# All chunks of a gated linear attention loaded as token pairs, with one decay sum for each pair of chunks

## The chip, the cores and the metric

The kernel runs on one core of a Trainium2 chip. The metric is the device time of one execution in microseconds (us); the median of three runs is given. The core has a matrix engine (PE, with weight loads listed apart as PEld), three engines for elementwise work (DVE, ACT, POOL), and SP, which here only issues DMA transfers. POOL can't read PSUM, where PE leaves its results.

## What is computed

A gated linear attention runs over 4 batches of 8 heads, 768 tokens and a head size of 48. Its output goes through a gated MLP that mixes along the sequence.

```python
for t in range(S):
    state = alpha[:, :, t, :, None] * state + np.einsum('bhd,bhe->bhde', k[:, :, t], v[:, :, t])
    y[:, :, t] = np.einsum('bhd,bhde->bhe', q[:, :, t], state)
...
h = np.maximum(x @ w_in, 0.0)
u, v = (h[..., :d_ff // 2].copy(), h[..., d_ff // 2:].copy())
v_n = (v - mu) / np.sqrt(var + 1e-06)
v_s = np.einsum('ts,bsd->btd', w_spatial, v_n) + b_spatial[None, :, None]
gated = u * v_s
return (gated @ w_out).astype(np.float32)
```

Here x is y with its heads joined to 384 columns, d_ff is 1024, and mu and var are taken over the 512 columns of v. Inputs and output are float32.

## The kernel before

**Chunks.** Each batch is cut into 6 chunks of 128 tokens, 24 chunks in all. Within a chunk the running product of alpha is B = exp(cumulative sum of ln alpha). With kt = k / B and qt = q * B, the scores are a plain product kt qt, masked so that a token sees only earlier ones and itself. The state between chunks is carried beside that.

**Two paths.** Chunks 0 to 7 (the tuple PAIRS names pairs 0 to 3) go through `pair` (L423), two chunks at once. Its loads (L441) put two neighbouring tokens in one partition, so that a packet has 384 bytes. The decay sum is four products of 384 columns for a pair (L461), two for the even tokens (par 0) and two for the odd ones. Each then has its own exponentials: `einvp` (L469, 1/B) and `eexpp` (L478, B, written back to PSUM). kt is L483, on POOL or DVE; qt is L490, on DVE, and reads B from PSUM. The transposes (L511) take 128 columns each.

Chunks 8 to 23 go through `first` (L634), one chunk at a time, with loads of one token to a partition in packets of 192 bytes (L646). There is one decay sum (L666) with four narrow products for the total decay (L669), one pair of exponentials (L678, L695), kt (L690, POOL), qt (L700, DVE, from PSUM), and transposes of 64 columns (L719).

Both paths then do the same steps. Scores are L583 or L754 and end in PSUM, where DVE multiplies them by the mask into `ptm` (L594, L765), four products of 512 columns for each two chunks. The masked scores times v are L610 or L782, the part from the carried state L623 or L776. State updates are L553 or L740: PE multiplies kt and v, DVE adds the old state (L339), POOL multiplies by the total decay (L344), and two casts write the state's blocks `sbd` (L351, L352, recorded at L199). `finish_x` (L356) copies the output to `x_sb`, transposes it and copies it to `xT`.

**The MLP.** `second_v` and `second_u` project a batch; relu evacuates to `v_sb` and `uT`. Statistics of v are on DVE (L893, L894), or on ACT for the four chunks of ACT_STATS; `vn` (L925) normalises. `second_s` multiplies by the transposed spatial weights, DVE adds the bias into `vsb` (L976), and POOL multiplies by u into `gT` (L989; on DVE three times at the end). `second_o` is the output product; its result is copied and stored by SP. All these matrix products are recorded at L828 and all copies at L197 (ACT) or L199 (DVE and POOL).

**Order.** Nothing is scheduled at run time. Every operation is appended to a list by the function that describes it, and the string PLAN names them in the order in which they are emitted: a letter for the engine and a number for the operation. `replay` (L109) goes through it. A number after a colon asks for a filling product of so many float32 columns on PE (L187) ahead of the operation, whose result is not used. Each engine works through its own instructions in this order and waits on semaphores. PSUM banks are handed out in rotation.

Of the kernel before, what the change touches and what calls it, by code (L numbers as in the profile page):

```python
# [14 lines left out]

class Op:


    def __init__(self, key, eng, dur, emit, deps=(), prio=0.0, take=None, lat=0.13, cols=0):  # L20
        self.key = key
        self.eng = {eng: dur} if isinstance(eng, str) else dict(eng)
        self.emit, self.prio, self.lat, self.cols = emit, prio, lat, cols
        self.take = [take] if isinstance(take, Slot) else list(take or ())
        self.deps = [d for d in deps if d is not None]
        self.done = False
        self.big = False


class Ring:  # L30


    def __init__(self, bufs):
        self.bufs = bufs


class Slot:
    def __init__(self, ring):
        self.ring, self.users = ring, []


ENGINES = {
    "kt": {"POOL": 0.9},
    "vb": {"POOL": 0.48, "ACT": 0.42},
    "S": {"POOL": 0.5},
    "sb": {"POOL": 0.73, "DVE": 0.95},
    "vn": {"DVE": 0.42},
    "xe": {"ACT": 0.4},
    "ev": {"DVE": 0.34, "ACT": 0.48},
    "u": {"ACT": 0.39, "DVE": 0.49},  # L50
    "o": {"ACT": 0.4},
}
PAIRS = (0, 1, 2, 3)
ACT_STATS = ((2, 2), (1, 4))
LETTERS = {"P": "PE", "D": "DVE", "A": "ACT", "G": "POOL", "S": "SP", "Q": "DMA"}

PLAN = """
S34 Q35 S36 Q37 G32 G0 Q33 S38 Q39 S94 Q95 S40 Q41 A42 P53:512:512:192 A54 D1 D2 D56 P43 S96 Q97 S98 Q99 S100 Q101
S163 Q164 S4 Q5 S165 Q166 S167 Q168 P59:464 G58 G48 A44 A45 A55 D46 D57 D47 P249:304 P49 P61 A50 P51 D52 D60 A62 A102
A250 P71:304 P74 P113 P103 D72 D73 D76 D75 P63 P77:172 D65 A114 D116 P119:148 A104 A64 A115 A105 A78 G66 G67 G106 D107  # L60
D117 D68 P79 P81 P111 P121 P247 P109 G3 G69 A108 A82 A80 D120 D122 D112 D110 P83 A84 A171 D248 S169 Q170 S9 Q10 S307
Q308 P131 P134 D133 D136 D132 D135 G70 G118 P172:228 P182 P123:240 A183 A8 A173 A124 P137 P138 A139 A174 G7 G6 D125
P85 G126 D128 D185 G127 G129 G175 P88 P142 P140 A86 A184 D176 D186 A143 A89 P188 P190 P180 P144 P178 A141 A191 A145
A181 P146 G11 G12 S309 Q310 S311 Q312 D130 D87 D179 D90 D189 P157 A187 A177 A158 A147 A13 P197 P200 P192 D199 D201
D198 D194 D202 P151:196 P155 A315 A193 A91 P326 P316 A327 P203 P153 P204 G195 G196 G329 A317 A328 A318 P149 A205 A154
D159 D156 D152 D330 G319 P208 P334 A209 P206 D320 P332 P324 P210 P322 D92 D335 D325 D333 D148 A207 P212 A211 A150 P347
P215 P221 A213 A160 A222 A216 S14 Q15 P223 P227 S18 Q19 D93 D323 D161 D348 D349 D214 G16 G17 A224 A228 P225 P229 A226
A21 P232 A234 D231 D230 D233 G20 P235:300 P238 S313 Q314 G331 G321 P344 P336 S367 Q368 S369 Q370 S22 Q23 S371 Q372
A237 A236 D217 D162 D346 A240 D338 A239 A218 D219 D220 A375 A337 P251 P263 P259 P376 A377 A378 G339 P264 D345 D341
D265 P260 D261 P255 P252 A380 A25 A24 D381 D253 P256 D257 G340 G342 G379 S409 Q410 S373 Q374 S446 Q447 S411 Q412 S413  # L70
Q414 S415 Q416 S26 Q27 S480 Q481 S448 Q449 S482 Q483 S450 Q451 S484 Q485 P383 A385 A417 S452 Q453 S577 Q578 S486 Q487
S581 Q582 S579 Q580 S583 Q584 P244 P241 P350 A246 D384 D245 D242 D243 P390 P354 P418 D392 D391 A351 A355 G262 G343
A420 A382 G254 G266 P279 P352 P271 P356 P393 P272 A353 A357 A419 G421 A422 A394 P280 P361 P386 P275 P395 A362 A424
A396 A31 D273 D423 D281 D387 P425 D397 D427 D426 D363 G282 G388 P276 P358 D277 P398 G258 G389 G278 G30 A399 A454 A359
A28 A488 P405 P432 P267 P455 P401 A402 A457 A456 D29 P291 P489 P268 A490 A459 D406 D433 D400 D434 D360 P283 P428 D269
D460 A492 D429 D493 G458 G491 P435 A284 A292 A436 G274 G461 G270 G430 G431 S648 Q649 S617 Q618 S650 Q651 S611 Q612
S652 Q653 S613 Q614 S690 Q691 S615 Q616 S694 Q695 S654 Q655 S692 Q693 P287 P462 P437 P495 P403 D463 D464 D497 D496
A288 A439 A438 P440 A585 A441 A364 D404 P469 P498 P295 P465 P586 P303 D471 D470 D466 D500 D499 A296 A587 A588 A590
A304 P299 G494 G467 G468 G589 G592 D591 D442 P472 A473 P501 P407 P474 A502 A300 P503 P593 P596 A443 A505 A408 D475
D476 P477 A478 D504 D366 D594 D595 D445 D444 D597 D365 P506 P600 P515 D601 D516 A507 A479 A508 D509 D602 A656 A510  # L80
A619 P517 P525 P513 P519 P529 P657 P533 P620 D511 D512 P526 P530 A514 A659 A658 A621 A661 A622 A698 A624 D518 D520
D527 D531 D662 P545 P534 P699 A701 A700 A703 D625 G598 G599 G660 G626 G623 G528 D535 P546 D547 P630 P627 P664 P537
P603 D631 D665 D704 G548 A629 A628 G632 G663 A604 P538 P634 P605 S728 Q729 S762 Q763 S696 Q697 S730 Q731 S732 Q733
S764 Q765 S766 Q767 D539 A607 A666 A606 D635 D636 P541 P667 P542 G702 G532 P706 P671 D668 D543 D673 D672 G669 G536
G670 G544 G633 P608 P637 P521 A707 A736 A708 A638 P737 P713 P639 P522 P549 D714 D715 D641 D523 A770 A609 A705 A738
A739 G740 A640 A741 D742 P771 P550 P642 A772 P709 P744 A774 A643 A746 D710 D551 D775 D745 D644 G524 S858 Q859 S734
Q735 S929 Q930 S860 Q861 G773 G711 G552 G712 G743 G540 P716 P674 A717 A675 P561 P718 P676 P777 P553 A562 A678 A677
D719 D779 D720 D610 P679 P751 A778 A554 A866 A680 A645 A681 P780 D752 P747 D748 D753 D781 D782 P682 P867 P721 P754
A868 A869 A871 A722 A755 S768 Q769 S862 Q863 A723 A776 D683 D872 P573 P688 P684 G749 G750 G870 P756 P874 D646 D757
D875 D685 D758 A689 A574 D724 A876 P686 P783 P569 P881 A784 P785 A570 A787 A687 A725 D882 D786 D883 P759 P557 A760  # L90
P788 P565 P796 P798 P800 S1042 Q1043 S971 Q972 S892 Q893 S864 Q865 S898 Q899 S896 Q897 A979 A558 A789 A566 A937 A900
S894 Q895 S935 Q936 G873 S975 Q976 S931 Q932 S933 Q934 S973 Q974 S977 Q978 S1008 Q1009 S567 Q568 S1046 Q1047 S559 Q560
S1012 Q1013 S1010 Q1011 S1044 Q1045 S1014 Q1015 D727 D647 D761 D726 P794 P806 D790 A791 D799 D797 D795 D792 D793 D801
P901 P980 P802 P938 P877 P807 A902 A903 A907 A905 A981 A939 A940 A982 A944 A984 P810 P803 A942 G904 D878 G941 G879
D808 D906 D804 G805 G880 G809 G983 D985 D943 P822 P884 P811 D812 A885 P823 P908 P886 P945 D824 P814 P911 P815 D912
D909 D816 G813 G817 G913 G825 A910 A887 A888 A947 A946 P889 A1016 A890 P952 P915 P987 D953 D916 D954 P830 P1017 P831
P818 A988 A1019 A1050 A1018 D917 P948 P819 P1051 D949 A1021 A986 A989 D1022 D832 G950 P834 A1052 G951 G1020 P990 P842
P918 A835 A1054 D820 D991 D1055 A843 A919 P838 P1024 P994 P920 D1025 D921 D995 D996 A839 A1023 G914 G833 G1053 G992
S1048 Q1049 S575 Q576 S836 Q837 S844 Q845 S293 Q294 S289 Q290 S571 Q572 S305 Q306 S301 Q302 S555 Q556 A922 A1026 S297
Q298 S285 Q286 S840 Q841 P826 P955 P827 D828 A956 P1057 P957 P1031 D958 P1027 D1028 D1033 D1032 P997 P923 A1058 A1059  # L100
A959 P969 P1060 A1056 A998 P999 D1062 D1001 D1061 D970 G821 G829 G993 G1029 A1000 A924 P960 P846 P1034 A961 A847 G1030
P1063 A1035 A1064 P1002 P963 P1036 P1065 D925 D891 A1003 D962 D1066 P850 P967 A1067 A1037 D1004 A926 D928 P1068 A964
A1038 P1039 D927 D968 A851 A1005 A1069 A1040 D1006 D1041 D1007 D1070 P965 P854 P1076 P1080 P1078 P1074 D966 A1079 A855
A1071 A1081 D1075 D1072 D1073 D1077 P1094 P1082 P1106 P1086 P1083 P1098 P1095 P1090 P1102 P1087 P1107 P1091 P1103
P1110 P1099 P1111 D1096 D1084 G1085 D1088 D1097 D1108 D1092 D1093 G1089 P1113 D1104 G1109 G1105 D1112 D1100 D1101
P1117 P1121 S852 Q853 S563 Q564 S856 Q857 S848 Q849 A1114 S1115 Q1116 A1118 P1133 S1119 Q1120 A1122 P1125 A1134 S1123
Q1124 P1129 S1135 Q1136 A1126 P1137 S1127 Q1128 A1130 A1138 S1131 Q1132 S1139 Q1140
"""


def replay(ops, fill, plan):

    for word in plan.split():
        number, *junk = word[1:].split(":")
# [9 lines left out]
def kernel(  # L124
# [50 lines left out]
    def bank(shape):  # L175
# [5 lines left out]
        for x in shape[1:]:  # L181
            n *= x
# [111 lines left out]
    def op(key, *args, **kw):  # L294
# [3 lines left out]
        for s in users:  # L298
            s.users.append(o)
# [857 lines left out]
```

## Time and profile before

| | |
|---|---|
| runs | 145.87, 145.33, 145.24 us; median 145.33 |
| profiled execution, span from first to last instruction | 142.7 us |
| median less span | 2.6 us |
| last causal mask on DVE ends | 119.4 us |
| POOL idle before `gT` L989 | 14.9 us, of which 13.5 after 119 us |
| DMA | 89,000 packets, 28.64 MB, 83,728 of them under 512 bytes |
| granted PE clock | 1.00 |

The span is that of one profiled execution; what lies around it is not in the profile, and the three runs were timed apart from it. Busy time of an engine is the time in which at least one of its records is open. Records of one engine can overlap, above all PE's, so a mean duration times a count exceeds what the engine needs. Where a price is wanted, the distance from one start to the next in an unbroken row is the better measure.

### The profile page before, as it was taken

What the parts mean: (1) busy time and instruction counts of PE and PEld (TensorE: products, weight loads), DVE (VectorE), ACT (ScalarE), POOL (GpSimd) and SP (SyncE); (2) the same over time, 40 slices, a digit from 0 to 9 for tenths busy, and PEclk for the clock granted to TensorE, in tenths of its full rate; (3) what the DMA queues carried; (4) which work ended last, traced back from release to release, by engine and by line L of the source; (5) the groups of instructions that cost most, each with busy time, mean ns of one, the idle gap of its engine ahead of it and who ended that gap; (6) DMA issues with size and microseconds to landing.
All of it is one profiled execution on the core that took longest, in us unless ns stands there. A gap on an engine that the chain in (4) does not pass through costs nothing.

```text
span 142.7 us, 4968 instructions
## 1 busy us (share of the span) xinstructions
PE 134.7 (94%) x1912; PEld 84.8 (59%) x1923; DVE 118.3 (83%) x291; ACT 109.3 (77%) x282; POOL 83.4 (58%) x146
## 2 busy tenths in 40 slices
PE   7999798899999999999999999999999989999990
PEld 3457575566577656675666665656666656566560
DVE  7279878989989699999998898989979779994940
ACT  3477759999888969889987999997978978940061
POOL 6703977366339776982389999410799993000720
PEclk9999999999999999999999999999999999999999
DMA  4999999999998999999999998999998794113045
GB/s 106 270 261 261 321 259 256 290 289 358 236 217 160 237 226 202 194 169 203 171 196 183 182 198 140 214 152 194 191 231 165 229 341 168 56 58 111 0 161 170
DMA packets 89000, 28.64 MB, mean 201 GB/s; under 512 B 83728, under 2 KB 87440, under 8 KB 88976
## 3 DMA queue, kind: packets, MB, share of 16 engines
q1 hardware_dynamic: 88944, 28.32, 91.3%
q8 instruction: 15, 0.25, 0.8%
q14 instruction: 9, 0.07, 0.2%
q0 software_dynamic: 32, 0.00, 0.0%
HBM read 23.60 MB, written 4.72 MB: 198 GB/s over the span
## 4 chain that ended last, share of the span: by engine, by line
PE 63%; SPq 9%; POOL 7%; DMA 6%; DVE 5%; ACT 4%; issue 3%; ACTq 0%; POOLq 0%; DVEq 0%
PE bank L828 46%; SPq L441 8%; DMA qc<-in_q_dram 6%; PE bank L719 2%; PE bank L754 2%; POOL kt L690 2%; POOL gT L989 2%; POOL sbd L199 2%; PE bank L782 2%; DVE ptm L765 1%; PE bank L740 1%; PE bank L666 1%; SPq L1081 1%; PE bank L776 1%; DVE qt L490 1%
## 5 line engine op out<-in xcount | busy, mean ns | idle before, releaser
L828 PE MATMUL bank<-w_spT,vn 128*128 128x384 bf16 x192 | 36.8, 326 | 0.0
L989 POOL TENSOR_TENSOR gT<-vsb,uT 128x384 bf16<-128x384 f32 x28 | 25.7, 925 | 14.9 <-DVE vsb L976 14.4
L765 DVE TENSOR_TENSOR ptm<-bank,mask 128x512 bf16<-128x512 f32 x32 | 20.7, 682 | 1.9 <-PE bank L398 1.2
L828 PEld LDWEIGHTS <-vn 128*128 128x128 bf16 x192 | 16.6, 97 | 9.5 <-issue 0.2
L690 POOL TENSOR_TENSOR kt<-kc,binv 128x384 bf16<-128x384 f32 x16 | 14.6, 915 | 9.9 <-ACT bc L685 5.1
L976 DVE TENSOR_TENSOR vsb<-bank,bsp_bc 128x384 f32<-128x384 f32 x31 | 16.5, 551 | 4.2 <-PE bank L828 2.5
L828 PE MATMUL bank<-xT,w_in 128*128 128x384 bf16 x96 | 18.7, 326 | 0.0
L828 PE MATMUL bank<-w_out_sb,gT 128*128 128x384 bf16 (+1 forms) x100 | 18.7, 319 | 0.0
L828 PE MATMUL bank<-w_in,xT 128*128 128x512 bf16 x61 | 17.1, 379 | 0.8 <-issue 0.2
L344 POOL TENSOR_TENSOR state<-state,bc 128x192 f32<-128x192 f32 x20 | 10.4, 522 | 8.9 <-ACT bc L559 3.4
L197 ACT COPY kqT<-bank 128x512 bf16<-128x512 bf16 x21 | 12.1, 598 | 3.7 <-PE bank L719 1.1
L199 POOL CAST sbd<-state 64x192 bf16<-64x192 f32 x38 | 13.3, 350 | 2.0
L893 DVE BATCH_NORM_STATS2 stats<-v_sb 128x6 f32<-128x512 bf16 x20 | 13.6, 682 | 0.3 <-ACT v_sb L203 0.3
L203 ACT ACTIVATE v_sb<-bank 128x512 bf16<-128x512 f32 x20 | 11.7, 604 | 1.2 <-PE bank L828 1.0
L828 PEld LDWEIGHTS <-w_in 128*128 128x128 bf16 x96 | 8.8, 97 | 5.9
L828 PEld LDWEIGHTS <-gT 128*128 128x128 bf16 x100 | 8.9, 97 | 5.6 <-DVE gT L989 0.4
L199 DVE COPY kqT<-bank 128x512 bf16<-128x512 bf16 x27 | 10.4, 416 | 1.9 <-PE bank L511 1.0
L197 ACT CAST x_sb<-bank 128x384 bf16<-128x384 f32 x24 | 11.4, 489 | 0.7 <-PE bank L610 0.2
L187 PE MATMUL bank<-junk 128*128 128x512 f32 (+9 forms) x24 | 10.5, 542 | 1.1 <-DVE junk L240 1.1
L197 ACT COPY xT<-bank 128x192 bf16<-128x192 bf16 (+1 forms) x26 | 9.3, 376 | 1.7 <-PE bank L398 1.1
L594 DVE TENSOR_TENSOR ptm<-bank,mask 128x512 bf16<-128x512 f32 x16 | 10.2, 682 | 0.5 <-PE bank L583 0.3
L197 ACT COPY o_sb<-bank 128x384 f32<-128x384 f32 x9 | 4.4, 484 | 8.0 <-PE bank L828 8.0
(126 smaller groups left out, 285.4 us busy)
## 6 DMA issues: line engine op xcount, KB each, us to landing
ac<-in_alpha_dram SPq DMA_DIRECT2D x16, 192.0 KB, 4.4
kc<-in_k_dram SPq DMA_DIRECT2D x16, 192.0 KB, 4.9
qc<-in_q_dram SPq DMA_DIRECT2D x16, 192.0 KB, 4.3
vc<-in_v_dram SPq DMA_DIRECT2D x16, 192.0 KB, 4.4
raw_w<-in_moe_w_spatial_dram SPq DMA_DIRECT2D x3, 768.0 KB, 6.7
out_dram<-raw_w SPq DMA_DIRECT2D x11, 192.0 KB, 2.7
out_dram<-o_sb SPq DMA_DIRECT2D x9, 192.0 KB, 1.9
ac<-in_alpha_dram SPq DMA_DIRECT2D x4, 384.0 KB, 6.2
```

Of the source, the lines that this page charges most:

```text
L187: nc.tensor.matmul(out=flat[:, 0:cols].rearrange("p (a b) -> p a b", a=4), lhsT=junk, rhs=junk[:, None, 0:n].to_broadcast([128, 4, n]), st ...
L197: nc.scalar.copy(out=out, in_=in_)
L199: ENG[eng].tensor_copy(out=out, in_=in_)
L203: nc.scalar.activation(out=out, in_=in_, func=AF.Relu)
L344: ENG[eng].tensor_tensor(out=st["state"], in0=st["state"], in1=st["bc"][:, :, None].to_broadcast([128, HP, D]), op=ALU.mult)
L441: nc.sync.dma_start(out=t.rearrange("p h a d -> p h (a d)"), in_=src[b, :, t0:t0 + 2 * C, :].rearrange("h (p a) d -> p h (a d)", a=2))
L690: ENG[eng].tensor_mul(out=k_blocks(kt3)[:, :, :, 0:D], in0=quad(st["kc"]), in1=st["binv"])
L765: nc.vector.tensor_tensor(out=st["ptm"][:, s], in0=st[f"pt{s}"], in1=mask4, op=ALU.mult)
L828: return lambda ps: nc.tensor.matmul(out=out(ps), lhsT=lhsT(), rhs=rhs(), start=start, stop=stop)
L893: nc.vector.bn_stats(out=stats, in_=d["v_sb"][:, tt, :])
L976: nc.vector.tensor_tensor(out=hold["vs"], in0=ps[:, 0:TH], in1=bsp_bc[:, th, :], op=ALU.add)
L989: ENG[eng].tensor_tensor(out=bt[b]["gT"][:, dsl, cols], in0=hold["vs"], in1=bt[b]["uT"][:, dsl, cols], op=ALU.mult)
```

## The change

The path for single chunks goes. All twelve pairs of chunks are loaded as pairs, two tokens to a partition in packets of 384 bytes.

For each pair there is one decay sum. The even token's alpha is multiplied by the odd one's (`pa`), in place, and the sum runs over the logs of these products, so it gives B of the odd token. The even token's k is multiplied by the odd alpha (`ka`), and its q by the inverse of the odd alpha (`qa`), which ACT makes as exp(-ln alpha) (`ia`); after that one 1/B and one B serve both tokens. B is written to SBUF (`bexp`), no longer back to PSUM, so kt and qt can each be done on POOL or DVE.

State updates write 64x64 tiles. The sum goes to its own buffer `zs`; the decayed state for the next chunk and the two blocks `sbd` are both products of `zs` with the decay. The mask is kept once for four heads and broadcast. All statistics of v are on DVE. The order table is new, with an explicit PSUM bank for every operation that takes one (after an @).

Engines by the new order table, for the operations that move: `pa`, `ka`, `qa` 31 on POOL and 5 on DVE; kt 12 and 12; qt 14 and 10; gT 15 and 16 (and the last one on DVE from PSUM, as before); states 11 and 5; state blocks 16 and 4 (each two products); v casts 12 on POOL, 9 on ACT, 3 on DVE. Filling products come to 2,096 columns, where they were 3,572. In SP's queue the first loads stand in the order alpha 0, q 0, alpha 1, k 0, v 0, alpha 2; before, alpha 0, k 0, q 0, alpha 1, v 0.

```diff
-PAIRS = (0, 1, 2, 3)
-ACT_STATS = ((2, 2), (1, 4))
...
-S34 Q35 S36 Q37 G32 G0 Q33 S38 Q39 S94 Q95 S40 Q41 A42 P53:512:512:192 A54 D1 D2 D56 P43 S96 Q97 S98 Q99 S100 Q101
...
+S52 G4 D1 D2 S54 D0 D56 A57 G7 S109 D3 G113
+A58 P61@0:512:512:360 A62 S53 A64 G60 S55 D59 A114 D68 D65 A63
...
+            def load(_, x=x, src=src):
+                nc.sync.dma_start(
+                    out=t[x].rearrange("p h a d -> p h (a d)"),
+                    in_=src[b, :, t0:t0 + 2 * C, :].rearrange("h (p a) d -> p h (a d)", a=2))
...
+        op(("pa", j), "POOL DVE", lambda e: mul(e, t["ac"][:, :, 0, :], t["ac"][:, :, 0, :], t["ac"][:, :, 1, :]),
+           [("ac", j)])
...
+            nc.scalar.activation(out=la[:, :, :, 0:D], in_=quad(t["ac"][:, :, 0, :]), func=AF.Ln)
...
+            nc.scalar.activation(out=ia[n2], in_=t["ac"][:, :, 1, :], func=AF.Ln)
+            nc.scalar.activation(out=ia[n2], in_=ia[n2], func=AF.Exp, scale=-1.0)
...
+        op(("ka", j), "POOL DVE", lambda e: mul(e, t["kc"][:, :, 0, :], t["kc"][:, :, 0, :], t["ac"][:, :, 1, :]),
+           [("ac", j), ("kc", j)])
+        op(("qa", j), "POOL DVE", lambda e: mul(e, t["qc"][:, :, 0, :], t["qc"][:, :, 0, :], ia[n2]),
+           [("ia", j), ("qc", j)])
...
-                for p2 in range(2):
-                    nc.tensor.matmul(
-                        out=cm[:, 0:DM], lhsT=lt_pair if p2 > par else le_pair, rhs=lap[:, p2, :, 0:D],
-                        start=(p2 == 0), stop=(p2 == 1))
...
+            nc.tensor.matmul(out=cm[:, 0:DM], lhsT=le_pair, rhs=la[:, :, :, 0:D], start=True, stop=True)
...
-                nc.scalar.activation(out=cv, in_=cv, func=AF.Exp)
...
+        op(("eexp", j), "ACT", lambda _: nc.scalar.activation(out=bexp[n2], in_=sums(), func=AF.Exp),
...
-            op(("qtp", j, par), "DVE", 0.47, qtf, got(("eexpp", j, par), ("qc", 2 * j), ("cz", 0)) + tr_users("q", jo), prio=P + 4, use=[sl_c[par]])
...
+            op(("qt", j, par), "POOL DVE",
+               lambda e, par=par: mul(
+                   e, qt[:, par, :, :, 0:D], quad(t["qc"][:, :, par, :]), quad(bexp[n2])),
...
-                            out=T[i]["tp"][:, hp, :], lhsT=k_window(ktp[rows, par], hp, 2 - 2 * s),
-                            rhs=st["vb"][rows, par, 2 * hp + s, :], start=(n == 0), stop=(n == 3))
...
+                                out=tp[i][half(s), hp, :], lhsT=kt[rows, par, hp, s, :],
+                                rhs=vbp[j % 3][rows, par, 2 * hp + s, :], start=(par == 0), stop=(par == 1))
...
+                op(("S", i), "POOL DVE", lambda e, i=i, decay=decay: mul(e, state[i % 3], zs[i % 3], decay(slice(0, 128))),
...
+                    mul(e, sbd[i % NB][half(s), :, s * D:s * D + D], zs[i % 3][half(s)], decay(half(s)))
...
+                        in1=mask[:, par][:, None, :].to_broadcast([128, HP, 128]), op=ALU.mult)
...
+        spare[d] = op(("g", b, d, th), "POOL DVE",
+                      lambda e: mul(e, gT[b % 2][:, d, cols], vs[d], uT[b % 3][:, d, cols]),
```

## What the time is predicted to be, and why

> **What bounds the kernel now.** I read the page first, then busy time in two stretches that meet where DVE ends its last causal mask (119.4 us), then the chain of waits, then the groups, then single instructions.
>
> ```profile
> PE 134.7 (94%) x1912; PEld 84.8 (59%) x1923; DVE 118.3 (83%) x291; ACT 109.3 (77%) x282; POOL 83.4 (58%) x146
> ```
>
> ```profile
> 0.00:119.40 119.40, 114.79 (x1769) 73.32 (x1780) 103.14 (x257) 99.64 (x256) 79.59 (x142) 1.00 1.06 223
> 119.40:142.70 23.30, 19.89 (x149) 11.46 (x146) 15.17 (x35) 9.70 (x27) 3.85 (x4) 1.00 0.25 88
> ```
>
> The columns are the length, then PE, PEld, DVE, ACT, POOL, the granted clock (full throughout), the DMA share and GB/s. In the first stretch PE idles 4.6 us, DVE 16.3, POOL 39.8. In the second PE works alone.
>
> ```profile
> PE 63%; SPq 9%; POOL 7%; DMA 6%; DVE 5%; ACT 4%; issue 3%; ACTq 0%; POOLq 0%; DVEq 0%
> ```
>
> ```profile
> 13.96 8.82 DMA qc<-in_q_dram
> ...
> 27.72 0.50 PE bank L553 x16
> ...
> 34.43 0.35 PE bank L583 x16
> ...
> 45.44 0.47 PE bank L610 x32
> ...
> 48.23 0.20 PE bank L782 x8
> ...
> 50.94 0.23 PE bank L719 x16
> ...
> 121.48 17.55 PE bank L828 x105
> ```
>
> The chain (start, length, what) is loads until 22.8 us, then mostly PE. The last row gives 0.167 us for a matrix product of 384 columns (17.55/105), although the groups call one 326 ns: records overlap. So I price an instruction by what it adds in a row, and PE's pieces by this chain.
>
> **What PE loses.** Four pairs take the paired path now. Their four sums of 384 columns become one: 3 x 0.163 (L461, start to start) x 4 pairs = 2.0 us. Their sixteen 128-column transposes (0.056 apart, 0.90) become two sets of sixteen at 0.23: 0.44 x 4 = 1.8. The eight pairs loaded as single chunks lose one 384-column sum and four narrow ones of 0.025 each: 0.26 x 8 = 2.1. Scores (two sets of 0.35 against two of 0.33) and the masked products (0.47 against two of 0.20 plus joining) are level. That is -5.9 us. The 64x64 state products do not occur before: thirty-two of them cost 0.50 like L553's, or 0.25 if four run at once, or 0.70 at L583's pace; I take 0.50, level, with +-2.5 us over twelve pairs. Filling products go from 3,572 to 2,096 columns, but stand in idle time: nothing.
>
> The order table also moves products behind the last mask. Counted in both tables and priced as above (v 0.65, u 0.49, output 0.65, each mixing product 0.163), PE has 20.7 us left there before and 26.4 after. So it loses 11.3 us in the first stretch and gains 5.7 in the second. The second took 23.3 us, 2.6 more than its products (last store and drain); with 26.4 it takes 29.0.
>
> **What DVE has in the first stretch.** In a row a mask costs 0.60 (four take 2.48), a 384-wide product 0.47 (two qt take 1.02, one 0.55), a k/q copy 0.33, statistics 0.86. Up to the last mask it gains 8 kt, 9 gT, 5 products with alpha (22 x 0.47 = 10.3), 5 states of 192 columns (0.27 each, 1.4), state blocks 1.6, 3 v casts 0.8, 4 statistics 3.4, 2 x copies 0.9. It loses 14 qt (6.6), 9 u (4.2), 6 vsb (2.8), 8 k/q copies (2.6), 5 smaller x copies (0.8), the bias copy and the sums of ACT's statistics (1.5), memsets (0.8). The sum is -0.9, within what I can count: DVE stays at 103 us. Behind the mask it gains 6.6, under PE's cover (15.2 + 6.6 < 29).
>
> **POOL.** 31 products with alpha and 14 qt at 0.88 (a gT to the next op) add 39.6; gT falls from 22 to 8 there (-12.3), kt from 20 to 12 (-7.0), state from 19 to 11 (-3.8). State blocks become products: 32 at 0.46 (L344's price; the cast's 0.36 is the other bound) for 34 casts at 0.36, +2.5. Six more weight casts +3.9, smaller masks -3.6. Sum +19.3: POOL goes from 79.6 to 99 us.
>
> ACT ends lower: half the exponentials of the sums (-9.4 at 0.39), no squares (-3.2), fewer casts and outputs (-7), against one log and one exponential more per pair (+5), k/q copies (+4) and u (+4.5).
>
> **DMA and SP.** Thirty-two load issues and 32,768 packets go. The chain has no load after 22.8 us, and the loads before that are paired already, so this buys nothing. One order does cost: k of the first pair goes from second in SP's queue to fourth. Paired loads land about 1.5 us apart, so kt waits for it 0 to 2 us; DVE, its masks and PE's filling products are behind. I put it inside the idle time below.
>
> **The wait that the change adds.**
>
> ```profile
> 132.73 2.02 POOL L989 TENSOR_TENSOR gT<-vsb,uT 128x384 bf16<-128x384 f32 x2
> ...
> 134.08 1.09 DVE L989 TENSOR_TENSOR gT<-vsb,uT 128x384 bf16<-128x384 f32 x1
> ```
>
> ```profile
> L989 DVE TENSOR_TENSOR gT<-vsb,uT x3: 547/559/1086, 132.6 to 136.6; 128x384 bf16<-128x384 f32 x3
> ```
>
> ```profile
> L199 POOL CAST sbd<-state x38: 337/341/618, 14.6 to 118.9; 64x192 bf16<-64x192 f32 x38
> ```
>
> A DVE product with both operands in SBUF, begun while POOL's gT ran to 134.75, took 1.09 us instead of 0.55 and ended 0.42 after POOL. POOL suffers too: a cast of 618 ns beside DVE's kt at 22.0, two gT in 2.02. Before, DVE runs only 7 such products (4 kt, 3 gT), since qt (L490, L700) reads PSUM. After, the exponential goes to SBUF, and DVE has 12 kt, 10 qt, 5 with alpha, 9 gT, 5 states and 8 state blocks: 49 before the last mask. If they fall at random, POOL is running at 99/116 = 0.85 of them; the rest of a 0.88 us op is 0.44 on average, of which 0.13 hides under DVE's own start (0.55 - 0.42). That is 0.85 x 0.31 x 49 = 13 us of DVE waiting. Bounds: 0 if the order keeps them apart, 20 if every one meets a fresh op. Behind a waiting product stand masks and PSUM reads, and PE waits for those. Nearly level engines (DVE 103, POOL 99, PE 114.8 - 11.3 = 103.5 by its overlapping records) mean that a wait lands on the path about one time in three: I take 4.3.
>
> **Sum.** First stretch: DVE 103, its idle first 10 us (4.5, from the page's slices), and 4.6 of other stalls, what the fullest engine PE has now: 112.1; waits 4.3; second stretch 29.0. Span 145.4 against 142.7. The runs' median of 145.33 is 2.6 over the span, so the time is **148.0 us**, 1.8% slower.
>
> **Rivals.**
> - *The port paces.* POOL's 99 and DVE's 49 x 0.42 = 20.6 exclude each other: 119 us plus 4.5 at the start, plus 29.0: span 152.7, 155.3 us. For it: both directions of waiting are seen. Against: POOL's own 0.05 to 0.1 between reads may overlap. The Trainium skill (SBUF — State Buffer, Who interferes with whom) says that a VectorE instruction with two SBUF inputs and a GpSimd one that reads SBUF exclude each other, the second waiting in full. The row at 134.08 agrees, with 0.42 us after the other's end.
> - *The waits hide.* Products meet POOL where DVE would idle: 112.1 + 29.0 + 2.6 = 143.7. For it: DVE idled 16 us in this stretch. Against: PE paced then.
> - *PE still paces, faster.* The other engines keep up as now: 142.7 - 11.3 + 5.7 = 137.1, 139.7 us; to 137 with the cheap state products. For it: PE is 63% of the chain and DVE's first stretch is no fuller than now. It decides if DVE's idle time and waits together stay under 119.4 - 11.3 - 103 = 5 us. Against it: the start alone takes 4.5, and POOL gains 19 us and feeds kt, qt and the decay sum.
> - *Nothing visible*: gain on PE and loss on the port cancel near 145.3.
>
> **Chances.** Forecast (146.1 to 152) 0.41; port 0.15; waits hide 0.17; PE paces 0.22; cancel 0.05. A measurement here tells 0.5% (144.6 to 146.1) from no change. Of the third case 0.13 lies below 144.6, 0.03 inside, 0.01 above: faster 0.35, same 0.08, slower 0.57. The range is 137 to 154; about 0.05 lies below and 0.1 above; the forecast's own is 146.1 to 152.
>
> **What would show it.** POOL near 100 us busy and DVE near 125; PE about 120; kt, qt and gT on DVE with medians well over 0.55 us and maxima near 1.1 to 1.4, POOL's products with maxima over 1.1; the share of DVE and POOL in the chain well over today's 12%; the last mask ending near 116 and PE alone for 29 us. It is wrong if DVE's products with two SBUF inputs stay at 0.55, or if PE keeps most of the chain and the last mask ends by 108; and if the first mask comes later than 13 us (10.9 now), the load order cost more than I took.

## The result, and the profile after

The changed kernel takes **169.15 us** (median of four runs, 167.87 to 169.97) against 145.3 before: the ratio is 1.164, with a 95% interval of 1.157 to 1.171. Forecast were 148.0 us and a range of 137 to 154. The direction was right and the size far off.

The page's busy time and the chain of waits of the kernel after:

```profile
PE 140.2 (84%) x2313; PEld 84.6 (51%) x2313; DVE 147.9 (89%) x298; ACT 107.3 (65%) x272; POOL 117.1 (70%) x155
...
PE 36%; DVE 34%; POOL 13%; issue 11%; ACT 4%; DVEq 0%; POOLq 0%
```

The two stretches, which now meet at 135.54 us, where DVE ends its last causal mask (length, then PE, PEld, DVE, ACT, POOL, the granted clock, the DMA share and GB/s):

```profile
0.00:135.54 135.54, 113.17 (x2098) 68.50 (x2098) 125.61 (x249) 96.46 (x243) 110.02 (x148) 0.92 0.77 190
135.54:166.10 30.56, 27.07 (x216) 16.11 (x215) 22.28 (x50) 10.81 (x29) 7.04 (x7) 1.00 0.28 98
```

Before, DVE had 103 us of work in the first stretch and idled 16. Now it is busy for 125.6 of 135.5 us. PE's share of the chain falls from 63% to 36%, and DVE and POOL together go from 12% to 47%. The second stretch is 30.6 us, near the 29.0 that were forecast. So nearly all of the miss lies in the first, which was forecast to end at 116.4 us (112.1 and 4.3).

What DVE does with the time is seen in one kind of product. The rows give count, then minimum, median and maximum in ns, and first and last start:

```profile
L205 DVE TENSOR_TENSOR kt<-kc,binv x12: 540/806/1343, 9.9 to 103.6; 128x384 bf16<-128x384 f32 x12
L205 POOL TENSOR_TENSOR kt<-kc,binv x12: 907/1021/1233, 16.4 to 124.8; 128x384 bf16<-128x384 f32 x12
```

The cheapest kt on DVE still takes 0.54 us, as before. Half of them take over 0.8. In the timeline, a pair whose two kt fall on both engines at once:

```profile
60.51 0.91 POOL L205 TENSOR_TENSOR kt<-kc,binv 128x384 bf16<-128x384 f32 x1
```

```profile
60.57 1.26 DVE L205 TENSOR_TENSOR kt<-kc,binv 128x384 bf16<-128x384 f32 x1
```

POOL's ends at 61.42. DVE's, begun 0.06 us after POOL's, ends at 61.83, 0.41 later: the same 0.42 that the row at 134.08 showed before the change.

Two things stand beside this. The first mask starts at 18.73 us (10.93 before), and PE's clock, full throughout before, is at half speed from 13.6 to 34.0 us:

```profile
PEclk9996555599999999999999999999999999999999
```

### The profile page after: what moved, and what is told of

Its sections match the earlier page's. It is cut to its first block, busy times and chain, and to the rows that moved or that the text cites. A ratio compares the mean times of both kernels' runs of the same rounds, so it can differ in the third digit from the quotient of the medians.

```text
span 166.1 us, 5703 instructions
## 1 busy us (share of the span) xinstructions
PE 140.2 (84%) x2313; PEld 84.6 (51%) x2313; DVE 147.9 (89%) x298; ACT 107.3 (65%) x272; POOL 117.1 (70%) x155
## 3 DMA queue, kind: packets, MB, share of 16 engines
q1 hardware_dynamic: 55664, 28.32, 66.9%
## 4 chain that ended last, share of the span: by engine, by line
PE 36%; DVE 34%; POOL 13%; issue 11%; ACT 4%; DVEq 0%; POOLq 0%
PE bank L566 24%; DVE ptm L503 7%; DVE vn L645 4%; POOL qt L205 4%; DVE sbd L205 3%; PE bank L495 3%; DVE kt L205 3%; DVE vs L701 2%; DVE gT L205 2%; DVE stats L628 2%; DVE qt L205 2%; POOL sbd L205 2%; POOL qc L205 2%; PE bank L532 2%; DVE state L205 2%
## 5 line engine op out<-in xcount | busy, mean ns | idle before, releaser
L205 POOL TENSOR_TENSOR gT<-vs,uT 128x384 bf16<-128x384 f32 x15 | 14.4, 967 | 21.9 <-DVE vs L701 19.5
L205 POOL TENSOR_TENSOR sbd<-zs,bc 64x192 bf16<-64x192 f32 x32 | 18.3, 571 | 4.3 <-DVE zs L469 3.1
L205 POOL TENSOR_TENSOR qt<-qc,bexp 128x384 bf16<-128x384 f32 x14 | 15.4, 1104 | 4.2 <-ACT bexp L394 2.9
L701 DVE TENSOR_TENSOR vs<-bank,bsp_bc 128x384 f32<-128x384 f32 x31 | 16.2, 547 | 1.9 <-PE bank L566 1.7
L194 ACT COPY xT<-bank 128x192 bf16<-128x192 bf16 x38 | 12.5, 392 | 2.9 <-PE bank L553 2.6
L645 DVE TENSOR_SCALAR vn<-v_sb,mvs,rstd 128x512 bf16<-128x512 bf16 x24 | 13.2, 574 | 1.2 <-ACT rstd L639 1.2
L200 ACT ACTIVATE uT<-bank 128x384 bf16<-128x384 f32 x26 | 12.5, 492 | 1.5 <-PE bank L566 1.5
L205 POOL TENSOR_TENSOR ac<-ac 128x384 f32<-128x384 f32 x9 | 9.3, 1029 | 5.6 <-DMA ac<-in_alpha_dram 5.5
L205 POOL TENSOR_TENSOR kt<-kc,binv 128x384 bf16<-128x384 f32 x12 | 12.3, 1027 | 0.6 <-ACT binv L392 0.5
L253 PE MATMUL bank<-junk 128*128 128x512 f32 (+7 forms) x22 | 10.7, 608 | 1.8 <-DVE junk L295 1.8
L205 POOL TENSOR_TENSOR qc<-qc,ia 128x384 f32<-128x384 f32 x11 | 11.9, 1086 | 0.2
```

Source lines behind the costliest of these rows:

```text
L194: nc.scalar.copy(out=out, in_=in_)
L200: nc.scalar.activation(out=out, in_=in_, func=AF.Relu)
L205: ENG[eng].tensor_tensor(out=out, in0=in0, in1=in1, op=ALU.mult)
L253: nc.tensor.matmul(out=t[:, 0:cols].rearrange("p (a b) -> p a b", a=4), lhsT=junk, rhs=junk[:, None, 0:n].to_broadcast([128, 4, n]), start ...
L645: nc.vector.tensor_scalar(out=vn[n2][:, x, :], in0=v_sb[n2][:, x, :], scalar1=mvs[n2][:, x, 0:1], scalar2=rstd[n2][:, x:x + 1], op0=ALU.su ...
L701: nc.vector.tensor_tensor(out=vs[d], in0=banks[sl.bank][:, 0:TH], in1=bsp_bc[:, th, :], op=ALU.add)
```

## The experiments

Four theories were put to the test. A: DVE's operations and POOL's reads of SBUF exclude each other, and DVE pays for it with path time. B: the half clock and the late start. C: the new order itself, or the number of operations, whatever one costs. D: a general slowness of SBUF.

### POOL reads nothing

```diff
+        elif eng == "POOL":
+            nc.gpsimd.memset(out, 0.01)
...
-    def mul(eng, out, in0, in1):
+    def mul(eng, out, in0, in1, fill=0.01):
+        if eng == "POOL":
+            for _ in range(2):
+                nc.gpsimd.memset(out, fill)
+            return
...
```

> The changed kernel, in which every product that POOL makes is replaced by two memsets of its output (every cast on POOL by one), so that POOL reads nothing from SBUF while it stays about as busy; POOL's products and casts are left out of what is computed. Theory A, collisions of DVE's and POOL's SBUF reads make up most of the 24 us: DVE's products with two SBUF inputs fall from means of 0.74 to 0.92 us back to 0.50 to 0.60, DVE's busy time from 147.9 to about 125 us, and the time to 145 to 153 us. Theory B, the clock at half speed from 13.6 to 34.1 us and the start make up most of it: the time stays at 160 us or more, though DVE's products are shorter. Theory C, the new order itself keeps the engines apart whatever an instruction costs: DVE's busy time falls by over 15 us but the time by less than 5.

149.21 us, ratio 1.025 (1.018 to 1.033). Its two stretches, which meet at its last mask:

```profile
0.00:116.44 116.44, 109.65 (x2098) 67.97 (x2098) 104.06 (x249) 94.00 (x243) 94.65 (x270) 0.91 0.89 221
116.44:147.00 30.56, 27.06 (x216) 16.04 (x215) 22.23 (x50) 10.93 (x29) 0.00 (x0) 1.00 0.28 98
```

and its products on DVE:

```profile
L211 DVE TENSOR_TENSOR kt<-kc,binv x12: 541/548/645, 9.5 to 90.7; 128x384 bf16<-128x384 f32 x12
...
L211 DVE TENSOR_TENSOR qt<-qc,bexp x10: 523/548/552, 16.0 to 106.8; 128x384 bf16<-128x384 f32 x10
```

Every product of 384 columns is back near 0.55 us (kt at most 0.645), and DVE has 104.06 us in the first stretch, 21.55 less. The last mask ends 19.1 us earlier. The second stretch is the same to 0.01 us. Theory A takes 20 of the 24 us. Two reservations: POOL is busy for 22 us less in this kernel (94.7 against 117.1), since two memsets take 0.86 us where a product takes 0.91 to 1.1; and `vn` still waits for some 2.5 us in it (24 with a mean of 0.514 us, 0.409 before the change).

The order table is the same here and the clock no better (0.91 in the first stretch, 0.92 in the changed kernel). So theories B and C are left with the 3.9 us by which this kernel is slower than the one before, as far as clock and order cost the same with the waits and without. Its chain is PE's again:

```profile
PE 68%; DVE 12%; DMA 7%; ACT 4%; POOL 3%; issue 2%; SPq 1%; DVEq 0%; POOLq 0%
```

### The products with alpha left out

```diff
-        op(("pa", j), "POOL DVE", lambda e: mul(e, t["ac"][:, :, 0, :], t["ac"][:, :, 0, :], t["ac"][:, :, 1, :]),
+        op(("pa", j), "POOL DVE", lambda e: None,
...
```

> The changed kernel without its 36 products with alpha (31 on POOL, 5 on DVE), which are left out of what is computed; order and everything else stay. POOL falls from 117 to about 84 us busy, DVE by 2.7 plus its waits. Theory A: collisions scale with POOL's reads: DVE's waiting falls from 21.5 to about 14 us and the time to 155 to 162 us. If POOL's chain through the products with alpha is what paces (POOL 13% of the chain), the time falls to 150 or less. If the collisions don't depend on how busy POOL is, 164 or more.

156.66 us, ratio 1.081 (1.074 to 1.089), inside the 155 to 162 of theory A. The first stretch:

```profile
0.00:124.54 124.54, 112.19 (x2098) 68.03 (x2098) 112.44 (x244) 95.28 (x243) 77.30 (x117) 0.92 0.84 206
```

Of DVE's 112.44 us, 101.3 are work (104.06 less five products of 0.55) and 11.1 waits, half of the 21.55 above, with POOL busy for 62% of the stretch instead of 81%. Even with 33 us less on POOL, the kernel is 8% slower than before the change.

### Two inputs, or one

```diff
-    def mul(eng, out, in0, in1):
+    def mul(eng, out, in0, in1, two=True):
+        if eng == "DVE" and two:
+            nc.vector.tensor_scalar(out=out, in0=in0, scalar1=0.95, scalar2=1.0, op0=ALU.mult, op1=ALU.mult)
+            return
...
```

> The changed kernel in which each of DVE's products with two SBUF inputs multiplies its first input by a constant instead (the second input is left out of what is computed, and of what the product waits for); POOL does all its work. Theory A as the two inputs: the DVE operations keep one duration, POOL's products fall from 1.03 to 1.10 to 0.91 to 1.00 us, and the time comes to 146 to 154 us. Theory A as any fast DVE read of SBUF (vn, with one input, grew from 0.41 to 0.57 us): these operations still show maxima of 0.9 us or more and the time stays above 158.

160.31 us, ratio 1.105 (1.098 to 1.112).

```profile
L208 POOL TENSOR_TENSOR qt<-qc,bexp x14: 991/1002/1111, 9.9 to 116.9; 128x384 bf16<-128x384 f32 x14
L206 DVE TENSOR_SCALAR qt<-qc x10: 327/889/1152, 16.8 to 118.1; 128x384 bf16<-128x384 f32 x10
```

With one input the operation is faster, 0.33 us undisturbed, and waits all the same: half of the q operations take 0.89 us or more. So two inputs are not the whole condition. The Trainium skill (SBUF — State Buffer, Who interferes with whom) names a second one in the same list as the first: `copy`, `cast` and `tensor_scalar` can contend as well, in a mode that uses two ports. This run agrees, as far as its speed tells the mode (0.33 us for 384 columns, where two inputs take 0.55; the trace doesn't name modes). Below, the fast mode means this. What the forecast left out on that ground is `vn`, a `tensor_scalar` from bf16 to bf16, whose mean went from 0.409 to 0.574 us, and the v casts on DVE.

The run also parts the two directions. POOL's q products go back to a median of 1.00 us, so POOL is hardly held up by these short operations, and the kernel is still 15 us slower than before the change. DVE waits about as long as in the changed kernel: what the groups take above their minimum comes to 4.1 us for kt, 4.4 for qt, 3.2 for gT and 4.0 for the state blocks. What the run saves is DVE's work; DVE's own waiting is what costs.

### The same collision put into the kernel before

```diff
-    outp = ctx.enter_context(tc.tile_pool(name="outp", bufs=4))
+    outp = ctx.enter_context(tc.tile_pool(name="outp", bufs=3))
...
+    bx_bufs = [consts.tile([128, H, D], BF16, name=f"bx{n}") for n in range(2)]
...
-            nc.scalar.activation(out=st["cv"], in_=st["cv"], func=AF.Exp)
+            st["bx"] = bx_bufs[i % 2]
+            nc.scalar.activation(out=quad(st["bx"]), in_=st["cv"], func=AF.Exp)
...
-            nc.vector.tensor_mul(out=qt[:, :, ::-1, 0:D], in0=quad(st["qc"]), in1=st["cv"])
+            nc.vector.tensor_mul(out=qt[:, :, ::-1, 0:D], in0=quad(st["qc"]), in1=quad(st["bx"]))
```

> The kernel before the change with one thing of the change put in: the exponential that q is multiplied by is written to SBUF (two bf16 tiles, for which one of the four output tiles goes), so that DVE's 24 q products read two SBUF inputs instead of one; order, loads and engines are as before. Theory A (two SBUF inputs on DVE against POOL's reads): the mean of qt on DVE goes from 0.55 to 0.75 to 0.95 us, POOL's kt and gT from 0.92 to 0.95 to 1.05, and since PE paces this kernel most of the 5 to 9 us on DVE is absorbed: 146 to 150 us. Theory D (SBUF bandwidth in general, or only the many more products of the change): qt stays within 0.05 of 0.55 and the time within 1 us.

152.09 us, ratio 1.049 (1.043 to 1.055). With two buffers, the q products of chunks 13 and 19 read the exponential of a later chunk and wait for it, 1.3 us of idle time on DVE together. The q products of chunks 8 to 23 before, then all of this run's:

```profile
L700 DVE TENSOR_TENSOR qt<-qc,bank x16: 541/544/554, 43.8 to 111.6; 128x384 bf16<-128x384 f32 x16
```

```profile
L703 DVE TENSOR_TENSOR qt<-qc,bx x16: 542/904/1265, 44.8 to 118.4; 128x384 bf16<-128x384 f32 x16
...
L492 DVE TENSOR_TENSOR qt<-qc,bx x8: 551/770/1264, 7.8 to 32.7; 128x384 bf16<-128x384 f32 x8
```

The operand's place and type (bf16 for float32) have changed, and one output tile fewer is there; order and loads are the old ones, and POOL is busy for 59% of the span. The median goes from 0.544 to 0.904 us, far outside the 0.05 that theory D allowed. DVE's busy time grows by 7.9 us (118.3 to 126.2) and the time by 6.7, of which up to 1.3 can be the waits for the later exponential. That is outside the expected 146 to 150, because I had again counted on PE's pace to absorb the waits. It absorbs little: PE's share of the chain falls from 63% to 35%, and DVE's rises from 5% to 20%.

### The clock and the start

More filling products on PE in the changed kernel, and the same without POOL's reads:

```diff
-S175 A115 S111 G5 S110 D67 G69 P118@1:512:16 S177 P50@2 S176 A119
+S175 A115 S111 G5 S110 D67 G69 P118@1:512:300 S177 P50@2 S176 A119
...
```

> The changed kernel with about 2,400 more columns of filling products on PE between 11 and 18 us, nothing else changed. Theory B, the half clock costs much: the granted clock stays full and the time falls by 5 us or more, to 164 us or less. Theory A: DVE paces there with or without a full clock, and the time falls by 3 us or less (166 to 170).

> Both together: POOL reads no SBUF (its products and casts are left out, memsets in their place) and PE has the additional filling products. Theory A: within 2 us of the run without POOL's reads alone. Theory B: 5 us or more below that run. If both add up on different stretches, it is below both single runs by what the other one brings.

169.04 us (ratio 1.156, 1.145 to 1.167) and 150.46 us (1.034, 1.027 to 1.042). The half clock was not removed, only shortened and moved, as the first one's clock shows:

```profile
PEclk9999597559999999999999999999999699999999
```

Mean granted clocks are 0.947 against 0.938 of the changed kernel, and 0.963 against 0.930 without POOL's reads. As an estimate from these means and the spans, the half clock lasts about 18 us instead of 21 in the first pair and 11 instead of 21 in the second. The time falls in neither, as theory A expected. The added products occupy PE too, so this is no price of the half clock. What rules theory B out as the cause of the 24 us is the run without POOL's reads, which takes 149.2 us with the half clock in it.

The loads:

```diff
-S52 G4 D1 D2 S54 D0 D56 A57 G7 S109 D3 G113
-A58 P61@0:512:512:360 A62 S53 A64 G60 S55 D59 A114 D68 D65 A63
+S52 G4 D1 D2 S53 S54 D0 D56 A57 G7 S109 D3 G113
+A58 P61@0:512:512:360 A62 A64 G60 S55 D59 A114 D68 D65 A63
```

> The changed kernel with the first pair's k issued second on SP's queue, as before the change, instead of fourth; nothing else changed. If the load order costs what the first k waits for, the first mask ends 1.5 to 3 us earlier than 18.7 us and the time falls by 1.5 to 3 us. If the start is paced by DVE's and POOL's products side by side, the first mask moves by less than 1 us and the time stays within 1 us.

170.10 us, ratio 1.168 (1.160 to 1.176), and the first mask is later, at 19.62 us. Both numbers lie inside the second expectation (0.9 us each, less than 1), but its reason is not what the trace shows, and neither expectation saw a delay coming. POOL's queue before 10 us, with k second:

```profile
9.22 0.99 POOL L205 TENSOR_TENSOR ac<-ac 128x384 f32<-128x384 f32 x1 [7.10 <-DMA ac<-in_alpha_dram]
10.18 0.98 POOL L205 TENSOR_TENSOR qc<-qc,ia 128x384 f32<-128x384 f32 x1
```

POOL's first product in its order is that of the second pair's alpha, whose load is now one place further back (in the changed kernel it starts at 7.62). The first pair's q stands behind it. SP's order and POOL's order belong together; here, moving one alone only moved the wait.

Last, the kernel before without its filling products:

```diff
-S34 Q35 S36 Q37 G32 G0 Q33 S38 Q39 S94 Q95 S40 Q41 A42 P53:512:512:192 A54 D1 D2 D56 P43 S96 Q97 S98 Q99 S100 Q101
+S34 Q35 S36 Q37 G32 G0 Q33 S38 Q39 S94 Q95 S40 Q41 A42 P53 A54 D1 D2 D56 P43 S96 Q97 S98 Q99 S100 Q101
...
```

> The kernel before the change without any of its filling products on PE, nothing else changed. If a clock at half speed in the first 30 us costs much, PE (63% of the chain there) shows it: granted clock 0.5 for some 10 to 20 us early and a time 3 to 10 us above 145.3. If PE is idle enough early to absorb it, the time stays within 1 us and the half clock of the changed kernel explains nothing.

146.03 us over ten runs, ratio 1.005 (1.002 to 1.008), with the clock at 0.998. The half clock never came, so this run says nothing on its price.

### Other orders, and products that read PSUM

The same operations as in the changed kernel, in an order worked out from the trace's prices so that the two engines keep apart; then with the q exponential back in PSUM; then with k's there too. Each has an order table of its own; shown are the first lines of the first table and the two operands:

```diff
-S52 G4 D1 D2 S54 D0 D56 A57 G7 S109 D3 G113
+D0 S109 S52 S53 S54 D113 D2 D56 A114 A57 D1 G4 P118@0:512:512:80 S55 G59
...
-        op(("eexp", j), "ACT", lambda _: nc.scalar.activation(out=bexp[n2], in_=sums(), func=AF.Exp),
+        op(("eexp", j), "ACT", lambda _: nc.scalar.activation(out=sums(), in_=sums(), func=AF.Exp),
...
-                   e, kt[:, par, :, :, 0:D], quad(t["kc"][:, :, par, :]), quad(binv[n2])),
+                   e, kt[:, par, :, :, 0:D], quad(t["kc"][:, :, par, :]), quad(inv())),
```

> The changed kernel with another order table and nothing else: the same operations, with orders and engines chosen so that DVE's operations with fast or two SBUF inputs and POOL's products and casts are not due at the same time by the durations in the trace of the run without POOL's reads (net prices: product 0.47 us on DVE, 0.87 to 0.95 on POOL); casts move from POOL to ACT (12 of 16 weights, 18 of 24 of v), and filling products come to 5,376 columns. Theory A: kt, qt and gT on DVE come back to medians of 0.55 and means under 0.65, and the time to 148 to 155 us, near the run without POOL's reads (149.2). Theory C, each instruction of the change costs what it costs and the order changes little: above 160.

> The changed kernel with the exponential for q written back to the bank of the sums, as before the change, so that all 24 q products are on DVE with one input in PSUM, and an order table chosen in the same way for that. Theory A: q products at 0.55 us throughout with maxima under 0.65, no matter what POOL does; POOL under 105 us busy; time 2 to 4 us below the reordered kernel that keeps it in SBUF: 144 to 151 us. If collisions no longer count once the order keeps them apart, both are within 1 us.

> As the run before it, and the exponential for k goes to a PSUM bank of its own too, so that all kt and qt are on DVE with one input in PSUM; order table chosen in the same way. Of DVE's products with two SBUF inputs 11 remain besides the statistics' vn (2 with alpha, 7 gT, 2 states). Theory A: DVE busy 125 to 132 us with hardly any waits, POOL 95 to 105, and 143 to 149 us, level with the kernel before the change or a little faster. If the whole design costs more apart from the port, 150 or more.

164.87 us (ratio 1.130, 1.124 to 1.136), 158.93 (1.091, 1.087 to 1.094) and 158.25 (1.086, 1.082 to 1.091). All three times miss what theory A had; the first and the third lie where their rivals were put (above 160, 150 or more). The first order brought the medians down (kt 0.560, qt 0.668, gT 0.559), but maxima are still 1.24 to 1.35 us. By the group means of the run without POOL's reads, some 10 us of waits are left of the 21.5. The table also gives DVE more to do, 270 instructions before the last mask instead of 249, and DVE is busy for 141 us. An order by precomputed times kept the two engines apart only in part; that small slips bring them together again is likely, but was not shown. Taking the operand out of SBUF kept them apart throughout. In the second run all 24 q products take 0.537 to 0.555 us. From the third:

```profile
PE 142.4 (91%) x2304; PEld 85.0 (54%) x2319; DVE 125.4 (80%) x293; ACT 111.5 (71%) x281; POOL 98.8 (63%) x151
```

```profile
L194 DVE TENSOR_TENSOR kt<-kc,bank x24: 535/547/555, 8.8 to 119.4; 128x384 bf16<-128x384 f32 x24
```

All 48 of DVE's kt and qt are between 0.535 and 0.555 us while POOL works for 99 us. That is 11 us better than the changed kernel, and still 13 worse than before. DVE is as lightly loaded as in the kernel without POOL's reads (125.4 against 126.3 us) and PE has as much of the chain (67% and 68%), but the last mask ends at 128.7 instead of 116.4 us. Of these 12.3 us, 2.4 come back behind it (28.2 us instead of 30.6). The half clock doesn't last longer here (about 18 us against 21, estimated as above), so it is not what sets the two apart, unless it costs more in this order. What else differs is the table, which also asks for 4,848 columns of filling products instead of 2,608. The clock was tried (two of seven changed words of the table):

```diff
-P306@7,1
+P306@7,1:160
...
-P363@3,1
+P363@3,1:192
...
```

> The run with kt and qt from PSUM, with 1,100 more columns of filling products on PE between 22 and 46 us. There the port is out of the way and PE is 67% of the chain, and its clock was at half speed from 27 to 42 us, with PE busy about 85% of that time by its records. If the half clock costs time once PE paces, a full clock there brings 3 to 7 us: 151 to 155. If it doesn't (what PE does there waits for others anyway), or if the filling products come in the way, 157 to 160 as without them.

158.72 us (1.089, 1.081 to 1.097), with the clock at 0.957 against 0.943, as the second expectation has it. The half clock lasts some 4 us less by the same estimate, and the time doesn't fall; PE is busy for 4.4 us more (146.8 against 142.4) and has 78% of the chain. Whether the added products take what the clock gives was not parted. What holds these orders back was not settled, and no version was found that beats the kernel before.

## Why the prediction was wrong, point by point

The kernels with the change's order table can be laid side by side: DVE's busy time in the first stretch and the end of the last mask.

| kernel | DVE waits beyond the first row's, us | DVE busy, us | last mask, us | difference |
|---|---|---|---|---|
| POOL reads nothing | 0 | 104.1 | 116.4 | 12.4 |
| no products with alpha | 11.1 | 112.4 | 124.5 | 12.1 |
| DVE with one input | not separated | 116.5 | 128.4 | 11.9 |
| the change | 21.5 | 125.6 | 135.5 | 9.9 |

The last mask ends 10 to 12 us after as much time as DVE is busy. Each microsecond by which DVE is busy longer than in the first row, waits included, puts the last mask off by 0.9 to 1. In the first row PE is as full as DVE (109.65 of 116.44 us, and 68% of the chain); with the waits DVE sets the pace.

- **DVE's work, 103 us: right.** It is 104.06 without POOL's reads, with 2.5 us in it that `vn` still waits.
- **The mechanism: right, and incomplete.** Products with two SBUF inputs wait for POOL's reads (a kt takes 0.55 us without them, 0.806 in the median with them). Operations in the fast mode (`vn`, casts) do so as well, and were not counted.
- **Waits of 13 us on DVE: too small.** They are 21.5. Group by group against the run without POOL's reads, the products with two inputs grow by 18.3 us over the whole span (kt 3.8, qt 3.6, gT 3.0, blocks 4.5, states 2.2, products with alpha 1.2). That is 0.33 us for each of 56, where I had 0.265 for 49. The rest is `vn` (1.5 more than there) and casts.
- **"A wait lands on the path about one time in three", 4.3 us: this is the step that failed.** Taking the waits out brings the last mask forward by 19.1 us for 21.5 us of waits, nine tenths. The argument was that three engines near 103 us share the pace. But the forecast itself had DVE at 103 of 112 us; an engine with 9 us of slack can't take 13 us of waits, let alone 21. The run with the collision put into the kernel before shows that even a pace set by PE covers little of it: 6.7 us for 7.9 us of longer products and 1.3 us of idle time.
- **Other stalls, 9.1 us of DVE's idle time: too small by 3.3** (116.44 - 104.06 = 12.4 without POOL's reads).
- **The load order, 0 to 2 us, inside the idle time: at its upper bound, and not all that was added to the start.** With the products with alpha left out, DVE's first kt waits for k until 9.15 us, where it began at 6.84 before: 2.3 us. But the first mask comes 7.8 us later than before, 4.5 without POOL's reads (15.39 against 10.93) and 3.5 without the products with alpha (14.40). The first pair's q products now run on POOL and end at 12.66 us in the changed kernel (on DVE at 9.35 before), and on DVE a state and its blocks stand ahead of the first mask. How the rest divides was not measured. The prediction's sign, a first mask after 13 us, appeared, but not for the load order alone.
- **The second stretch, 29.0 us: 30.56.** PE's share was 27.1 of it, for a forecast of 26.4.
- **PE loses 11.3 us in the first stretch: not confirmed.** Its terms add up to 11.6 (5.9 and 5.7); the slip doesn't reach the time. Without POOL's reads PE is busy for 109.65 us there, where 103.5 were expected, but some 20 us of it run at half clock, which the prediction did not foresee. Price and clock were not parted.
- **POOL, 99 us in the first stretch: 110.** In the run with one input, where POOL is hardly held up, it is 103.5. So some 4.5 us look like price (a product of two float32 operands takes 0.99 us, not the 0.91 of kt and gT from which I took it) and the rest like its own waits for DVE.
- **DMA buys nothing: right.** The share of the DMA engines' time that queue q1 takes falls from 91.3% to 66.9%, and the time doesn't follow; the chain has no load in it.
- **Filling products cost nothing: right within what these runs show.** The kernel before is 0.5% slower without its 3,572 columns, and 2,444 more in the changed kernel leave the time as it is. The new table has 2,608 columns, not the 2,096 that I counted.
- **The signs.** DVE's medians (kt 0.806, qt 0.754, gT only 0.592), its maxima and the chain shares came as named. The busy times named there were too low, and don't follow from the prediction's own terms, which give DVE 138 us (103, 13 and 21.8) instead of 125 and PE 129 (103.5 and 25.6) instead of 120. Measured are 147.9 and 140.2.

The sum of the span, then: 14.8 us from waits on the path, 4.3 from the undisturbed first stretch (DVE 1.1, idle 3.3) and 1.6 from the second make the 20.7 between 145.4 and 166.1.

The rival "the port paces" had the right sign and 155.3 us (its terms add up to 155.7). It priced POOL's work plus DVE's share of the port, and took DVE's other work to fit in the gaps. With DVE nearly full, its other work has to wait in line too; by the table above that is how the time comes out.

## What to carry to other kernels

Before an operand moves from PSUM to SBUF, list which of DVE's operations then have two SBUF inputs or a fast mode, and how long POOL reads SBUF beside them; price each at the rest of POOL's instruction, here a third of a microsecond. Then look at the slack of the engine that waits: here it was busy for 90% of the stretch, and nine tenths of the waits reached the end time. An operand in PSUM avoided the collision in all 48 cases here; an order that kept the engines apart on paper took away only about half of the waits.

## What was not expected of the hardware

**A memset on POOL delays DVE's fast mode, but not its two-input products.** In the kernel where POOL reads nothing, from DVE's and POOL's timelines:

```profile
64.50 1.15 DVE L651 TENSOR_SCALAR vn<-v_sb,mvs,rstd 128x512 bf16<-128x512 bf16 x1
```

```profile
64.01 1.13 POOL L196 MEMSET w_out_sb<- 128x384 bf16 x3
65.09 1.27 POOL L209 MEMSET gT<- 128x384 bf16 x3
```

`vn` takes 1.15 us beside memsets, 0.38 at best, while kt and qt stay at medians of 0.548 throughout that kernel. The Trainium skill (SBUF — State Buffer, Who interferes with whom) has it this way too: two inputs contend with a GpSimd operation that reads, the two-port modes with any.

**The half clock outlasts a busy PE.** In the kernel without POOL's reads the clock is at half speed from about 12 to 32.5 us, although PE has records open for at least 1.95 us of every 2 from 14 to 24 us. The Trainium skill (TensorE: Matmul & The Clock Gate, Part 1) gives about 3.4 us of sustained work until the clock is full again. By this trace that isn't enough, at least as a busy PE is counted in it.
